# Spreading a decode-attention kernel's softmax steps over three units of work, with small products and copies moved to ScalarE

## The chip, the cores and the metric

The kernel runs on one core of one Trainium2 chip. The metric is the device time of one execution in microseconds (us); each kernel has several runs. A run comes with the span of its profile (first to last instruction), the granted TensorE clock, and a state: "slow" when it is over 1.5% above the fastest run of the same kernel. "TensorE" does the matrix products, "VectorE" and "ScalarE" the elementwise work; in profile lines they are PE (with PEld for weight loads), DVE and ACT. SP is the engine that only issues the large transfers.

## The reference, cut to what matters

Eight sequences (batch 8), one new token each. Attention with 16 query heads on 8 key/value heads of width 256 over the last 1024 cached positions, beside a small MLP, mixed by a gate:

```python
q = (x @ wq) ...                                  # 8 x 16 heads x 256
scores = einsum("bhqd,bhkd->bhqk", q, k) * Dh**-0.5
p = softmax(scores);  o = einsum("bhqk,bhkd->bhqd", p, v)
a = o.reshape(B, Sq, Hq*Dh) @ wo
b = gelu(layernorm(x) @ w1 + b1) @ w2 + b2
return g * a + (1 - g) * b                        # g = sigmoid(sum(x * gate_w))
```

The cached keys and values are by far the largest input: 67 MB of 77.7 MB.

## The kernel before

Work is cut into 16 units (`NQ`): four key/value heads of one sequence each. A unit needs a 2 MB slot of keys and a 2 MB slot of values, which arrive in a ring of nine slots, in the order of use. A slot's buffer can be refilled when its last reader is done. Per unit: VectorE transposes the keys in four pieces (two halves of two); TensorE makes the scores in two halves of eight matmuls; the row maximum is found and shared (`top`, `share`); ScalarE takes exp; VectorE transposes the result (`turn`); TensorE multiplies with the values (`values`), and the result is combined (`gather`) and brought into place (`finish`). The excerpt leaves out allocations and bookkeeping.

```python
def turn(u):
    E, rowsum = soft.pop(u)
    ET = opool.tile(...)
    nc.vector.transpose(ET..., E...)
    selr = epool.tile([P, RQ], F32, ...)
    nc.vector.tensor_scalar_mul(selr[:], sel[:], rowsum[:])
    sm = ps_sm.tile([P, RQ], F32, tag="sm", name="sm")
    nc.tensor.matmul(sm[:], lhsT=ones_f[:], rhs=selr[:], start=True, stop=True)

def invert(u):
    nc.vector.reciprocal(rb[:], sm[:])
    nc.vector.tensor_tensor(rsel[:], rb[:], sel2[:], op=ALU.mult)

def gather(u):
    nc.vector.tensor_scalar_mul(os_[:], PO[:, 0, :], own[:, 0:1])
    nc.vector.scalar_tensor_tensor(os_[:], in0=PO[:, 1, :], scalar=own[:, 1:2],
                                   in1=os_[:], op0=ALU.mult, op1=ALU.add)

def finish(u):
    for j in range(NJ):
        nc.tensor.matmul(sm[:, j, :], lhsT=os_[:, j::NJ], rhs=rsel[:], ...)
    nc.vector.tensor_copy(oT[...], sm[:])          # the "oT copy"

# ... the start: MLP weights, then query weights; then
hs = mlp_hidden()
query()
for hf in range(NH):
    scores(0, hf)
mlp_out(hs)                                        # ends with a VectorE product, mixb
for u in range(1, NQ):
    for piece in range(CH // PIECE):
        turn_keys(u, 0, piece)
    scores(u, 0)
    top(u - 1)
    turn_keys(u, 1, 0)
    share(u - 1)                                   # with exp on ScalarE
    turn_keys(u, 1, 1)
    if u >= LAG:
        values(u - LAG)
    scores(u, 1)
    turn(u - 1)
    if u >= LAG:
        gather(u - LAG)
    invert(u - 1)
    if u >= LAG:
        finish(u - LAG)
# ... the last unit, then the projection with wo, and the output
```

This is the order in which each engine is given its instructions.

## Time and profile before

| | before |
|---|---|
| time, median of 3 runs | 211.6 us (211.46 to 214.57) |
| span of the profile | 210.8 us |
| busy: TensorE, VectorE, ScalarE | 140.1, 148.1, 29.7 us |
| mean granted TensorE clock | 0.83 of full |
| bytes moved, and rate in the loop | 77.7 MB, 2 MB slot each 4.89 us (428 GB/s) |
| last packet of the weights | 186.6 us |

From the page's part 2, the kernel before: each digit is the busy share, in tenths, of one of 40 slices of 5.3 us; PEclk is the granted TensorE clock in tenths of full.

```profile
PE   0069629575958676595959595958595858673771
DVE  7876140949697979979797979796969687883320
PEclk9999999858888789978888887879797969696555
DMA  5999999999999999999999999999999999910000
```

The transfers look like the limit: nine tenths and more until slice 35. But after them comes a tail of 24 us, in which only computing is left. So computing is behind. The chain of waits (the work that ended last, followed backwards; columns are start, length, engine, what was written, source line) shows one unit of the loop, kernel before:

```profile
168.60 2.24 DVE kt L358 x2
170.88 3.37 PE S L431 x8
174.40 0.17 DVE nmx L453
174.66 1.47 ACT E L456 x2
176.15 0.71 DVE ET L469
176.98 0.40 DVE os__1435 L506
177.40 0.50 DVE os__1435 L507
177.94 0.65 PE sm L522 x4
178.62 0.23 DVE oT L525
178.84 2.24 DVE kt L358 x2
```

From 168.60 to 178.84 us it is 10.24 us. The second line's first half of the scores (`S`, eight matmuls) takes 3.37 us, 0.42 us per matmul; the second half, off this chain, takes 1.91, 0.24 per matmul. The view of stretches tells why; its columns are the stretch, TensorE's busy time, weight loads, VectorE, ScalarE, GpSimd, then granted clock, DMA share and GB/s. Kernel before, three windows of 3.41 us and the next:

```profile
119.28:122.69 3.41, 3.00 (x8) 1.03 (x8) 2.84 (x4) 0.00 (x0) 0.00 (x0) 0.50 0.99 416
122.69:126.11 3.42, 2.99 (x27) 1.45 (x27) 2.45 (x5) 1.47 (x2) 0.00 (x0) 1.00 1.02 436
126.11:129.52 3.41, 1.37 (x9) 0.97 (x8) 2.96 (x7) 0.00 (x0) 0.00 (x0) 1.00 1.02 432
129.52:132.93 3.41, 2.99 (x8) 1.02 (x8) 2.85 (x4) 0.00 (x0) 0.00 (x0) 0.50 0.97 413
```

In the third window TensorE works 1.37 of 3.41 us, with one pause of 2.31 us that begins in it; in the fourth the clock is at half, and all eight score matmuls of the half unit begin in it. The trace's clock records repeat 6.83 us at full and 3.41 us at half: together 10.24 us, the pitch of the loop. From here on "window" is only a name for a stretch of 3.41 us (the lengths of these records, but for the last, are multiples of it), "gate", in the recorded texts, for the falls of the granted clock to 0.50, and "warm" and "cold" mean granted 1.00 and 0.50. Why the clock falls the records don't say.

### The profile page before, as it was taken

How to read it: one execution, taken by the hardware profiler on the slowest of the kernel's cores; microseconds unless marked ns; L12 is line 12 of the kernel's file. 1: busy time of each engine (PE TensorE's matmuls, PEld its weight loads, DVE VectorE, ACT ScalarE, POOL GpSimd, SP SyncE). 2: the span in 40 equal slices, each digit the busy share in tenths (PEclk: the TensorE clock that was granted, in tenths of full speed). 3: DMA queues.
4: the chain of work that ended last, by engine and by line, in shares of the span. 5: the costliest groups of instructions: out<-in, count | busy, mean ns of one | idle time of the engine just before them, and what ended most of it. 6: DMA issues, size and time to landing. Idle time of an engine off the chain costs nothing.

```text
span 210.8 us, 2528 instructions
## 1 busy us (share of the span) xinstructions
PE 140.1 (66%) x1013; PEld 70.6 (34%) x1022; DVE 148.1 (70%) x282; ACT 29.7 (14%) x40; POOL 0.8 (0%) x7
## 2 busy tenths in 40 slices
PE   0069629575958676595959595958595858673771
PEld 0066304231524333332324242424141424232361
DVE  7876140949697979979797979796969687883320
ACT  2210220020202112020202020202020202022000
POOL 1000000000000000000000000000000000000000
PEclk9999999858888789978888887879797969696555
DMA  5999999999999999999999999999999999910000
GB/s 225 411 437 420 432 420 431 429 420 435 423 429 435 417 438 420 429 432 423 429 429 423 434 426 417 441 417 429 435 423 435 432 410 418 404 54 0 0 3 4
DMA packets 6733, 77.84 MB, mean 369 GB/s; under 512 B 945, under 2 KB 1346, under 8 KB 1986
## 3 DMA queue, kind: packets, MB, share of 16 engines
q1 hardware_dynamic: 6512, 77.67, 87.1%
q8 instruction: 7, 0.11, 0.2%
q10 hardware_dynamic: 210, 0.02, 0.1%
q14 instruction: 4, 0.03, 0.0%
HBM read 77.68 MB, written 0.01 MB: 368 GB/s over the span
## 4 chain that ended last, share of the span: by engine, by line
PE 46%; DVE 38%; ACT 10%; issue 3%; ACTq 0%
PE S L431 27%; DVE kt L358 17%; ACT E L456 8%; PE sm L522 5%; DVE ET L469 4%; PE PO L493 3%; DVE oT L525 2%; PE Sq L374 2%; PE A_ps L656 1%; PE hT L545 1%; PE hT L535 1%; PE mz L451 1%; DVE qw L416 1%; DVE nmx L453 1%; DVE mx L443 1%
## 5 line engine op out<-in xcount | busy, mean ns | idle before, releaser
L431 PE MATMUL S<-kt,qw 128*128 128x512 bf16 x256 | 81.9, 476 | 44.2 <-DVE kt L358 39.2
L358 DVE STREAM_TRANSPOSE kt<-slot 128x1024 int32<-128x1024 int32 x64 | 77.1, 1226 | 0.0
L431 PEld LDWEIGHTS <-qw 128*128 128x128 bf16 x256 | 28.7, 112 | 86.8 <-issue 67.8
L456 ACT ACTIVATE E<-S,nmx 128x1024 bf16<-128x1024 f32 x16 | 22.6, 1412 | 140.1 <-DVE nmx L453 140.1
L493 PE MATMUL PO<-slot,ET 128*16 128x512 bf16 x256 | 20.2, 444 | 0.0
L443 DVE TENSOR_REDUCE mx<-S 128x1 f32<-128x1024 f32 x16 | 19.0, 1187 | 0.0
L469 DVE STREAM_TRANSPOSE ET<-E 128x512 int32<-128x512 int32 x16 | 11.4, 711 | 8.0 <-ACT E L456 8.0
L453 DVE TENSOR_REDUCE nmx<-mz 128x1 f32<-128x4 f32 x16 | 2.6, 160 | 12.9 <-PE mz L451 12.9
L451 PEld LDWEIGHTS mz<-m,same 128*128 128x128 f32 x32 | 7.4, 235 | 6.6 <-issue 3.9
L425 PE MATMUL S<-place,foreign 128*128 128x512 bf16 x23 | 9.2, 400 | 0.0
L476 PEld LDWEIGHTS sm<-selr,ones_f 128*128 128x128 f32 x32 | 6.4, 204 | 5.3 <-issue 3.1
L525 DVE CAST oT<-sm 128x16 bf16<-128x16 f32 x16 | 3.6, 226 | 6.3 <-PE sm L522 6.2
L493 PEld LDWEIGHTS <-ET 128*16 128x16 bf16 x256 | 5.6, 95 | 5.5 <-issue 2.7
L425 PEld LDWEIGHTS <-foreign 128*128 128x128 bf16 x32 | 4.8, 149 | 7.0 <-issue 6.9
L476 PE MATMUL sm<-selr,ones_f 128*128 128x8 f32 x32 | 4.9, 226 | 2.7 <-DVE selr L474 2.7
L451 PE MATMUL mz<-m,same 128*128 128x4 f32 x32 | 5.1, 230 | 1.7 <-DVE m L445 1.7
L482 DVE RECIPROCAL rb<-sm 128x8 f32<-128x8 f32 x16 | 3.3, 207 | 3.7 <-PE sm L476 3.6
L595 DVE TENSOR_SCALAR mixb<-bb,gg_s 128x112 f32<-128x112 f32 x1 | 0.3, 333 | 6.4 <-PE bb L591 6.4
L241 PE MATMUL tp<-ident,y_sb 8*128 8x8 bf16 x3 | 0.2, 170 | 6.9 <-DVE y_sb L302 6.9
L416 DVE CAST qw<-qp 32x1024 bf16<-32x1024 f32 x2 | 2.4, 1224 | 2.9 <-ACT qw L414 2.9
L445 DVE TENSOR_SCALAR m<-block,mx 128x4 f32<-128x4 f32 x16 | 3.7, 229 | 0.6
L374 PE MATMUL Sq<-slot,xT 128*8 128x512 bf16 x32 | 3.7, 621 | 0.0
(152 smaller groups left out, 93.8 us busy)
## 6 DMA issues: line engine op xcount, KB each, us to landing
slot<-in_A_v_cache_dram SPq DMA_DIRECT2D x16, 2048.0 KB, 24.9
slot<-in_A_k_cache_dram SPq DMA_DIRECT2D x15, 2048.0 KB, 29.4
slot<-in_A_wo_dram SPq DMA_DIRECT2D x3, 896.0 KB, 19.3
slot<-in_A_k_cache_dram SPq DMA_DIRECT2D x2, 1024.0 KB, 7.1
slot<-in_A_wq_dram SPq DMA_DIRECT2D x1, 2048.0 KB
slot<-in_B_w_dram SPq DMA_DIRECT2D x1, 1568.0 KB
slot<-in_B_w_dram SPq DMA_DIRECT2D x1, 1344.0 KB, 9.8
slot<-in_A_wq_dram SPq DMA_DIRECT2D x1, 1024.0 KB
```

What stands on the lines that cost most here:

```text
L358: nc.vector.transpose(KT[u, hf][:, c0 : c0 + PIECE] .rearrange("p c k x r -> p (c k x r)") .bitcast(WORD), kn[:, o : o + PIECE * Dh].bitca ...
L374: nc.tensor.matmul(Sq[32 * t : 32 * t + NB, n * QN : (n + 1) * QN], lhsT=xT[:, r + half, :], rhs=w[:, o + c : o + c + QN], start=(r == 0), ...
L425: nc.tensor.matmul(S[u][:, cols], lhsT=foreign[:], rhs=place[:], start=True, stop=False)
L431: nc.tensor.matmul(S[u][:, cols], lhsT=qw[:, j, u, m * RQ : m * RQ + P], rhs=kt[:, :, k, :, par], start=False, stop=(k == NK - 1 and par = ...
L443: nc.vector.reduce_max(mx[:], S[u][:], axis=AXIS.X)
L451: nc.tensor.matmul(mz[:], lhsT=same[:], rhs=m4[:], start=True, stop=True)
L456: nc.scalar.activation(E[:].rearrange("p c x i -> p c i x"), S.pop(u)[:].rearrange("p (c i x) -> p c i x", i=PAIR, x=BLK), ACT.Exp, bias=n ...
L469: nc.vector.transpose(ET[:].rearrange("p c r i -> p (c r i)").bitcast(WORD), E[:].rearrange("p c x i -> p (c x i)").bitcast(WORD),)
L476: nc.tensor.matmul(sm[:], lhsT=ones_f[:], rhs=selr[:], start=True, stop=True)
L493: nc.tensor.matmul(PO[32 * t : 32 * t + PAIR * RQ], lhsT=ET[:, c, 0:RQ, :], rhs=vn[:, PAIR * c * Dh : PAIR * (c + 1) * Dh], start=(c < QUA ...
L522: nc.tensor.matmul(sm[:, j, :], lhsT=os_[:, j::NJ], rhs=rsel[:], start=True, stop=True)
L525: nc.vector.tensor_copy(oT[:, half * RQ : (half + 1) * RQ, :, b].rearrange("p h j -> p j h"), sm[:])
```

## The change

Its intent: take VectorE work out of the unit, spread one unit's softmax over three (scores in unit u, exp at the end of u+1, its transpose in u+2, combining in u+3), so that no engine waits for a step just started; and start the query earlier. The core of the diff:

```diff
     add_kv("k", A_k_cache, 0, parts=2)
-    add(("w1",), rows_loader([w1_m, w1_t]))
     add(("wq", 0), ...)
     add(("wq", 1), ...)
+    add(("w1",), rows_loader([w1_m, w1_t]))
...                                            # keys transposed in one piece per half
-        selr = ...; nc.vector.tensor_scalar_mul(selr[:], sel[:], rowsum[:])
-        nc.tensor.matmul(sm[:], lhsT=ones_f[:], rhs=selr[:], ...)
+        nc.tensor.matmul(den[u][:], lhsT=rowden[:], rhs=rowsum[:], ...)     # total()
...
-        nc.vector.reciprocal(rb[:], sm[:])                                  # 128x8
-        nc.vector.tensor_tensor(rsel[:], rb[:], sel2[:], op=ALU.mult)
+        nc.vector.reciprocal(rb[:], den.pop(u)[:])                          # 128x1
+        nc.scalar.activation(rsel[u][:], sel2[:], ACT.Copy, scale=rb[:])
...
+        nc.scalar.activation(first[:], PO[:, 0, :], ACT.Copy, scale=own[:, 0:1])  # in values()
-        nc.vector.tensor_scalar_mul(os_[:], PO[:, 0, :], own[:, 0:1])
...
-        nc.vector.tensor_copy(oT[...], sm[:])
+        nc.scalar.copy(oT[...], sm[:])
...
-        nc.vector.tensor_scalar_mul(mixb[:], bb[:], gg_s[:, 1:2])
+        nc.scalar.activation(mixb[:], bb[:], ACT.Copy, scale=gg_s[:, 1:2])
...
-    hs = mlp_hidden()
     query()
+    hs = mlp_hidden()
...
     for u in range(1, NQ):
+        turn_keys(u, 0); scores(u, 0)
+        gather(u - LAG - 1); turn(u - LAG); total(u - LAG); finish(u - LAG - 1)
+        top(u - 1); share(u - 1)                   # the shared maximum, without exp
+        turn_keys(u, 1); values(u - LAG); invert(u - LAG)
+        scores(u, 1)
+        expo(u - 1)                                # exp
```

Also, the large clearing of `qw` moves to GpSimd, and the query's copies are split into eight.

More of the change, by code (lines that the diff above doesn't have):

```diff
@@ L77 @@
     BLK = 32
-    PIECE = 8
     BIG = 1e30
@@ L195 @@
     make_identity(nc, ident[:])
-    ones_f = consts.tile([P, P], F32)
-    nc.gpsimd.memset(ones_f[:], 1.0)
     Sq = ps_s.tile([P, W], F32, tag="S", name="Sq")
@@ L217 @@
     yT = consts.tile([P, NX, NB], BF16)
-    sel = consts.tile([P, RQ], F32)
+    rowden = consts.tile([P, P], F32)
     sel2 = consts.tile([P, RQ], F32)
@@ L250 @@
     by_row = ident[:].rearrange("p (b r) -> p r b", b=QUAD)
-    nc.vector.reduce_sum(sel[:], by_row[:, 0:RQ, :], axis=AXIS.X)
     nc.vector.reduce_sum(block[:], by_col, axis=AXIS.X)
@@ L257 @@
         zrow[:].rearrange("p (o r) -> p o r", o=1).to_broadcast([P, QUAD, BLK]),
+    )
+    nc.vector.tensor_copy(
+        rowden[:].rearrange("p (b r i) -> p b r i", b=QUAD, i=PAIR),
+        zrow[:, 0 : BLK // PAIR]
+        .rearrange("p (o r v) -> p o r v", o=1, v=1)
+        .to_broadcast([P, QUAD, BLK // PAIR, PAIR]),
     )
@@ L288 @@
             )
-    nc.vector.memset(qw[:], 0.0)
+    nc.gpsimd.memset(qw[:], 0.0)
     def norm_and_gate():
@@ L348, with turn_keys @@
     KT = {}
-    def turn_keys(u, hf, piece):
+    def turn_keys(u, hf):
         kn = slot("k", u)
-        if piece == 0:
-            KT[u, hf] = ktpool.tile(
-                [P, CH, NK, BLK, NPAR], BF16, tag="kt", name="kt"
-            )
-        c0 = piece * PIECE
-        o = (hf * CH + c0) * Dh
+        kt = ktpool.tile([P, CH, NK, BLK, NPAR], BF16, tag="kt", name="kt")
+        KT[u, hf] = kt
         nc.vector.transpose(
-            KT[u, hf][:, c0 : c0 + PIECE]
-            .rearrange("p c k x r -> p (c k x r)")
-            .bitcast(WORD),
-            kn[:, o : o + PIECE * Dh].bitcast(WORD),
+            kt[:].rearrange("p c k x r -> p (c k x r)").bitcast(WORD),
+            kn[:, hf * CH * Dh : (hf + 1) * CH * Dh].bitcast(WORD),
         )
-        if (hf + 1) * CH == NCK and c0 + PIECE == CH:
+        if hf == NH - 1:
             done()
@@ L410, in query @@
             rows = slice(BLK * b, BLK * (b + 1))
-            dst = qw[rows, :, :, BLK * b : BLK * (b + 1)]
-            src = qp[rows].rearrange("p j u m q -> p j u (m q)")
-            if b % 2 == 0:
-                nc.scalar.copy(dst, src)
-            else:
-                nc.vector.tensor_copy(dst, src)
+            for j in range(NJ):
+                dst = qw[rows, j, :, BLK * b : BLK * (b + 1)]
+                src = qp[rows, j].rearrange("p u m q -> p u (m q)")
+                if j == 0:
+                    nc.scalar.copy(dst, src)
+                else:
+                    nc.vector.tensor_copy(dst, src)
     S = {}
@@ L451, in share, with expo @@
         nc.tensor.matmul(mz[:], lhsT=same[:], rhs=m4[:], start=True, stop=True)
+        soft[u] = mz
+    def expo(u):
+        mz = soft.pop(u)
         nmx = epool.tile([P, 1], F32, tag="nmx", name="nmx")
@@ L467, in turn @@
         E, rowsum = soft.pop(u)
-        ET = opool.tile([P, NCK // PAIR, BLK, PAIR], BF16, tag="ET", name="ET")
+        ET = epool.tile([P, NCK // PAIR, BLK, PAIR], BF16, tag="ET", name="ET")
         nc.vector.transpose(
@@ L472, in turn, with total @@
         )
-        selr = epool.tile([P, RQ], F32, tag="selr", name="selr")
-        nc.vector.tensor_scalar_mul(selr[:], sel[:], rowsum[:])
-        sm = ps_sm.tile([P, RQ], F32, tag="sm", name="sm")
-        nc.tensor.matmul(sm[:], lhsT=ones_f[:], rhs=selr[:], start=True, stop=True)
-        soft[u] = (ET, sm)
-    def invert(u):
-        ET, sm = soft.pop(u)
-        rb = epool.tile([P, RQ], F32, tag="rb", name="rb")
-        nc.vector.reciprocal(rb[:], sm[:])
-        rsel = opool.tile([P, RQ], F32, tag="rsel", name="rsel")
-        nc.vector.tensor_tensor(rsel[:], rb[:], sel2[:], op=ALU.mult)
-        soft[u] = (ET, rsel)
+        soft[u] = (ET, rowsum)
+    den = {}
+    def total(u):
+        ET, rowsum = soft.pop(u)
+        den[u] = ps_sm.tile([P, 1], F32, tag="sm", name="den")
+        nc.tensor.matmul(
+            den[u][:], lhsT=rowden[:], rhs=rowsum[:], start=True, stop=True
+        )
+        soft[u] = ET
+    rsel = {}
+    def invert(u):
+        rsel[u] = opool.tile([P, RQ], F32, tag="rsel", name="rsel")
+        rb = epool.tile([P, 1], F32, tag="rb", name="rb")
+        nc.vector.reciprocal(rb[:], den.pop(u)[:])
+        nc.scalar.activation(rsel[u][:], sel2[:], ACT.Copy, scale=rb[:])
     def values(u):
-        ET, rsel = soft.pop(u)
+        ET = soft.pop(u)
         vn = slot("v", u)
@@ L500, in values @@
         done()
-        soft[u] = rsel
+        first = epool.tile([P, Dh], F32, tag="first", name="first")
+        nc.scalar.activation(first[:], PO[:, 0, :], ACT.Copy, scale=own[:, 0:1])
+        soft[u] = first
     def gather(u):
-        rsel = soft.pop(u)
+        first = soft.pop(u)
         os_ = epool.tile([P, Dh], F32, tag="os", name="os_")
-        nc.vector.tensor_scalar_mul(os_[:], PO[:, 0, :], own[:, 0:1])
         nc.vector.scalar_tensor_tensor(
@@ L510, in gather @@
             scalar=own[:, 1:2],
-            in1=os_[:],
+            in1=first[:],
             op0=ALU.mult,
@@ L514, in gather @@
         )
-        soft[u] = (os_, rsel)
+        soft[u] = os_
     def finish(u):
         b, half = divmod(u, Hkv // QUAD)
-        os_, rsel = soft.pop(u)
-        sm = ps_sm.tile([P, NJ, RQ], F32, tag="sm", name="sm")
+        os_, rs = soft.pop(u), rsel.pop(u)
+        sm = ps_sm.tile([P, NJ, RQ], F32, tag="sm", name="fin")
         for j in range(NJ):
             nc.tensor.matmul(
-                sm[:, j, :], lhsT=os_[:, j::NJ], rhs=rsel[:], start=True, stop=True
+                sm[:, j, :], lhsT=os_[:, j::NJ], rhs=rs[:], start=True, stop=True
             )
-        nc.vector.tensor_copy(
+        nc.scalar.copy(
             oT[:, half * RQ : (half + 1) * RQ, :, b].rearrange("p h j -> p j h"), sm[:]
@@ L594, in mlp_out @@
         done()
-        nc.vector.tensor_scalar_mul(mixb[:], bb[:], gg_s[:, 1:2])
+        nc.scalar.activation(mixb[:], bb[:], ACT.Copy, scale=gg_s[:, 1:2])
     norm_and_gate()
     for hf in range(NH):
-        for piece in range(CH // PIECE):
-            turn_keys(0, hf, piece)
+        turn_keys(0, hf)
+    query()
     hs = mlp_hidden()
-    query()
     for hf in range(NH):
@@ L606 @@
     for u in range(1, NQ):
-        for piece in range(CH // PIECE):
-            turn_keys(u, 0, piece)
+        turn_keys(u, 0)
         scores(u, 0)
+        if u >= LAG + 1:
+            gather(u - LAG - 1)
+        if u >= LAG:
+            turn(u - LAG)
+            total(u - LAG)
+        if u >= LAG + 1:
+            finish(u - LAG - 1)
         top(u - 1)
-        turn_keys(u, 1, 0)
         share(u - 1)
-        turn_keys(u, 1, 1)
+        turn_keys(u, 1)
         if u >= LAG:
             values(u - LAG)
+            invert(u - LAG)
         scores(u, 1)
-        turn(u - 1)
-        if u >= LAG:
-            gather(u - LAG)
-        invert(u - 1)
-        if u >= LAG:
-            finish(u - LAG)
+        expo(u - 1)
     u = NQ - 1
+    turn(u - 1)
+    total(u - 1)
     top(u)
     share(u)
+    gather(u - 2)
+    finish(u - 2)
+    invert(u - 1)
+    expo(u)
+    values(u - 1)
     turn(u)
-    values(u - 1)
+    total(u)
+    invert(u)
     gather(u - 1)
-    invert(u)
     A_ps = ps_misc.tile([P, DO], F32, tag="misc", name="A_ps")
```

## The prediction

The forecast's sum: 162.6 + 10 + 16 us is about 188.5 for the projection's end; with 0.4 and 4.1 the span is 193, and with 0.8 the time is 194 us. Two figures of its work per unit are estimates. The 2.26 us of a merged transpose is a straight line through the trace's 0.71 and 1.23 us (measured in the changed kernel: 2.31). ScalarE's added 1.0 us was measured there as 0.47 + 0.30 + 0.23 us (half of the combining, rsel, oT copy).

> **What bounds the kernel now.** The timeline shows a steady loop of 10.24 us per unit (score matmuls of successive units start at 119.69 and 129.94 us). The chain of waits runs through it serially: two key transposes 2.24, scores 3.37, sharing the maximum, exp 1.47, E transpose 0.71, combining 0.9, finishing 0.65, copy 0.23, then the next transposes. VectorE is busy about 8.9 of the 10.24 us; the rest is waiting inside this chain. The first eight score matmuls run 427 ns apart, the second eight 239 ns: TensorE stands idle 2.3 us before them and is halved for the next 3.41 us window (granted clock about 0.83). [...]10.24 us is exactly three windows.
>
> Under it lies a floor. The DMA row is at nine tenths until 184 us; a 2 MB slot takes 4.89 us (428 GB/s[...]). Two slots per unit are 9.79 us. All 77.7 MB land by about 186 us, and nothing the change does moves that. Unit 15's keys land at about 162 us but are transposed only at 178.8: the loop starts at 37 us (keys landed at 29) and loses 0.45 us per unit. So the prize is the 24 us after the last byte.
>
> **What the change does, per unit.** VectorE loses: the selr product 0.19, rsel product 0.17, first half of combining 0.48, the oT copy 0.23, and a fixed part of each merged transpose (1.23 for 1024 words, 0.71 for 512, so about 2.26 for 2048 against 2.45: 0.4 in all). Sum 1.4: 8.9 becomes 7.5 us. ScalarE gains about 1.0 us (estimate: one 128x256, two small operations) on 1.6. More important, the order: exp is started at a unit's end and its result transposed only one half later; gathering and finishing move one unit on. No VectorE step then waits for a fresh exp or finish. Compute alone could go at about 7.5 to 8.5 us per unit, below the 9.79 us of DMA.
>
> **Start.** Query weights first: queries need wq, landing about 4 us earlier, and no longer wait for the MLP; unit 1 starts near 30 us instead of 37. Compute catches up within about five units and then waits for keys.
>
> **End.** Unit 15 starts near 162.6; its iteration takes about 10, the epilogue (two value steps, finishes, spreading, 3.1 us of projection) about 16, so projection ends near 188.5; the last weights land at 186 to 187. Then 0.4 us and the 4.1 us of output seen now: span about 193. Runs read about 0.8 us above the span: **194 us**, range **191 to 200**.
>
> Chances: faster 0.96, same 0.03, slower 0.01.
>
> **What would show it.** DMA still at nine tenths and about 428 GB/s to about 186 us, with only some 6 to 8 us after it; VectorE transposes now waiting for the key slots' DMA, 1 to 2 us per unit from about unit 4 on; starts of units 9.8 us apart late, about 8 early; VectorE busy near 120 us; landing times from issue up towards 34 us.
>
> **What would make it wrong.** The halved clock: if TensorE's waits for DMA keep one window in three cold, and a cold score half plus the shared maximum (it waits for ScalarE's oT copy for its PSUM buffer) exceeds 9.8 us, the loop locks again at 10.24 us: then about 202.

## More of the kernel before

One more line matters, from the groups (line, engine, operation, count, busy us and mean ns, idle time just before and its releaser). Kernel before:

```profile
L595 DVE TENSOR_SCALAR mixb<-bb,gg_s 128x112 f32<-128x112 f32 x1 | 0.3, 333 | 6.4 <-PE bb L591 6.4
```

VectorE stands 6.4 us before the loop to make one 0.3 us product for the MLP.

## The result, and the profile after

The changed kernel's median was 195.28 us (4 runs, 192.88 to 196.14, two of them slow) against 211.53 us before. The ratio is 0.9165, 95% interval 0.9068 to 0.9262. Here and below a ratio is the mean time of one kernel's fast runs over that of the other's in the same rounds, so it isn't quite the ratio of the medians.

The same rows of part 2, changed kernel (40 slices of 4.8 us):

```profile
PE   0035999794878489857666699859684999396773
DVE  7876465995949494949493949494949585865310
PEclk9999657999699966999999558979998599997558
DMA  5999999999999999999999999999999999999980
```

The transfers now run almost to the end, and VectorE's row alternates. What it waits for is in the waits (engine, line, releaser: total us, times, longest us), changed kernel:

```profile
DVE kt L356 <- DMA slot<-in_A_k_cache_dram: 35.8, 14, 3.0
```

The timeline of VectorE has two successive units; the bracket is the idle time and its releaser:

```profile
133.91 2.31 DVE L356 STREAM_TRANSPOSE kt<-slot 128x2048 int32<-128x2048 int32 x1 [2.40 <-DMA slot<-in_A_k_cache_dram]
...
143.69 2.31 DVE L356 STREAM_TRANSPOSE kt<-slot 128x2048 int32<-128x2048 int32 x1 [2.79 <-DMA slot<-in_A_k_cache_dram]
```

The pitch is 9.78 us, two slots of 4.89 us. Each unit starts when its keys land. The start of the first key transposes of some units, read from the two traces, in us:

| unit | 1 | 2 | 3 | 6 | 10 | 15 | last projection matmul | span |
|---|---|---|---|---|---|---|---|---|
| keys landed (changed) | 29.4 | 34.4 | 44.2 | 73.7 | 112.9 | 162.1 | (weights: 186.3) | |
| before | 37.3 | 48.0 | 58.0 | 86.6 | 127.5 | 178.7 | 206.4 | 210.8 |
| changed | 31.0 | 36.8 | 45.6 | 75.0 | 114.3 | 163.3 | 187.9 | 191.1 |

The landing row is worked out from the packet records, adding up their bytes in order. By unit 3 the changed kernel is only 1.4 us behind the keys, and stays about there. The chain that ended last is the transfers up to unit 15, then the end of the kernel:

```profile
124.17 39.13 DMA slot<-in_A_k_cache_dram
163.31 2.32 DVE kt L356
...
184.87 3.00 PE A_ps L671 x126
187.89 0.33 DVE res L688
```

The last projection matmul ends 1.6 us after the weights' last packet. So the 24 us tail has become 5 us.

### The profile page after: what moved, and what is told of

The parts are those of the page before. It is cut to its first block, busy times and chain, and to the rows that moved or that the text cites. A ratio compares the mean times of both kernels' runs of the same rounds, so it can differ in the third digit from the quotient of the medians.

```text
span 191.1 us, 2508 instructions
## 1 busy us (share of the span) xinstructions
PE 135.0 (71%) x1022; PEld 69.5 (36%) x1022; DVE 128.0 (67%) x186; ACT 43.1 (23%) x91; POOL 5.0 (3%) x7
## 4 chain that ended last, share of the span: by engine, by line
DMA 84%; PE 7%; DVE 3%; ACT 3%; SPq 1%; issue 1%
DMA slot<-in_A_k_cache_dram 77%; DMA slot<-in_A_wq_dram 7%; PE fin L530 2%; PE A_ps L671 2%; ACT E L457 1%; PE PO L500 1%; DVE kt L356 1%; PE S L428 1%; DVE ET L470 1%; SPq L118 1%; DVE mx L440 1%; ACT first L509 0%; PE mz L448 0%; ACT oT L533 0%; PE pp L655 0%
## 5 line engine op out<-in xcount | busy, mean ns | idle before, releaser
L356 DVE STREAM_TRANSPOSE kt<-slot 128x2048 int32<-128x2048 int32 x32 | 73.7, 2305 | 35.8 <-DMA slot<-in_A_k_cache_dram 35.8
L428 PE MATMUL S<-kt,qw 128*128 128x512 bf16 x256 | 71.0, 424 | 29.9 <-DVE kt L356 27.6
L533 ACT CAST oT<-fin 128x16 bf16<-128x16 f32 x16 | 3.6, 227 | 82.2 <-PE fin L530 82.2
L509 ACT ACTIVATE first<-PO,own 128x256 f32<-128x256 f32 x16 | 7.6, 473 | 28.6 <-PE PO L500 28.5
L422 PE MATMUL S<-place,foreign 128*128 128x512 bf16 x32 | 13.4, 418 | 0.1
L481 PEld LDWEIGHTS den<-rowsum,rowden 128*128 128x128 f32 x32 | 7.2, 231 | 4.5 <-issue 1.4
L481 PE MATMUL den<-rowsum,rowden 128*128 128x1 f32 x32 | 5.2, 233 | 0.0
L492 ACT ACTIVATE rsel<-sel,rb 128x8 f32<-128x8 f32 x16 | 4.7, 296 | 0.7 <-DVE rb L491 0.7
L413 DVE CAST qw<-qp 32x512 bf16<-32x512 f32 x4 | 2.7, 687 | 3.2 <-ACT qw L411 3.2
L291 POOL MEMSET qw<- 128x5120 bf16 x1 | 4.4, 4364 | 0.0
## 6 DMA issues: line engine op xcount, KB each, us to landing
slot<-in_A_v_cache_dram SPq DMA_DIRECT2D x16, 2048.0 KB, 36.8
```

The costliest lines, as they stand in the source:

```text
L291: nc.gpsimd.memset(qw[:], 0.0)
L356: nc.vector.transpose(kt[:].rearrange("p c k x r -> p (c k x r)").bitcast(WORD), kn[:, hf * CH * Dh : (hf + 1) * CH * Dh].bitcast(WORD),)
L422: nc.tensor.matmul(S[u][:, cols], lhsT=foreign[:], rhs=place[:], start=True, stop=False)
L428: nc.tensor.matmul(S[u][:, cols], lhsT=qw[:, j, u, m * RQ : m * RQ + P], rhs=kt[:, :, k, :, par], start=False, stop=(k == NK - 1 and par = ...
L481: nc.tensor.matmul(den[u][:], lhsT=rowden[:], rhs=rowsum[:], start=True, stop=True)
L492: nc.scalar.activation(rsel[u][:], sel2[:], ACT.Copy, scale=rb[:])
```

## The experiments

Eleven kernels ran, in three groups; each group shares its runs of the kernel before, on one chip (medians before: 211.47, 213.0 and 213.05 us). The record's verdict is "faster" for e1, e5, e6, e7 and e8, "same" for e4, "unclear" for the third group (e9 to e11), in which five of the eleven runs of the kernel before were slow, and none for the single runs e2 and e3. All results passed the comparison with the reference. That says little for two of them (e2 and e3), which are wrong and passed too: the comparison doesn't resolve that part.

### e1: the changed kernel again

No edit.

> The changed kernel once more, unaltered, to see its spread and what moves in it. My theory (it is held by the transfers): unit starts 9.79 us apart from unit 3 on, last slot landed at about 186 us, span 191 to 194.5, times 192.5 to 196.5. A rival (its loop is still held by compute, which only happens to be near 9.8 us): in some runs the pitch differs from 9.79 us and vector transposes don't wait for key slots.

Measured: 194.37 us median (4 runs, 192.52 to 195.67), ratio 0.9175. From unit 3 on the pitch was 9.78 to 9.80 us, the last packet at 186.4, the last projection matmul at 187.5. The result repeats, with a spread of 3 us that e10 and e11 look into.

### e2 and e3: a quarter of the values, in both kernels

```diff
-        n = NCK * Dh // parts
+        n = NCK * Dh // parts // cut            # cut = 4 for values, 1 for keys
...
-        rhs=vn[:, PAIR * c * Dh : PAIR * (c + 1) * Dh],
+        rhs=vn[:, PAIR * t * Dh : PAIR * (t + 1) * Dh],     # t = c % 4
```

The work of the engines stays the same; the transfers shrink from 77.7 to 52.5 MB.

> The changed kernel, loading only a quarter of each value slot (and using that quarter four times; the result is wrong on purpose). Per unit the transfers then need about 6.1 us instead of 9.79. Theory (transfers hold the changed kernel; its compute alone goes at 7.5 to 8.5 us per unit): pitch falls to 7.5 to 8.5 us, unit 15 starts near 143 us, time about 171 us (167 to 178). Rival (compute holds it near 9.8 us): time stays above 190 us.

> The kernel before with the same cut of the value slots (wrong on purpose). Theory (its loop of 10.24 us is a chain of computing steps, and the transfers, though nine tenths busy, don't hold it): pitch stays 10.24 us, time 209 to 214 us. Rival (its transfers at nine tenths hold it): the time falls by 10 us or more.

Measured, e2: one run, 155.14 us (state unknown). The pitch fell to 6.90 us, below the 7.5 to 8.5 us I had expected. Part 2 and VectorE's timeline of e2:

```profile
DVE  7987524599999999999999999999999999663200
PEclk9999999999999999999999999999999999997558
...
91.58 2.29 DVE L356 STREAM_TRANSPOSE kt<-slot 128x2048 int32<-128x2048 int32 x1
98.48 2.29 DVE L356 STREAM_TRANSPOSE kt<-slot 128x2048 int32<-128x2048 int32 x1
```

VectorE is busy 6.86 of the 6.90 us, and in the loop TensorE's clock stays full. The transfers are not what holds e2: unit 15's keys landed at 114.7 us and were first transposed at 126.1. So 6.90 us per unit is the changed kernel's own pace, and the 9.79 us of the real one are the transfers'.

Measured, e3: one run, 214.75 us, span 213.0, clock 0.809 (state unknown). That is longer than any uncut run on its chip (spans of 208.1 to 211.3 us). The trace shows where: from unit 2 on its pitch was never under 10.2 us, where the profiled run of the kernel before had pitches of 9.05 to 10.02 us between units 2 and 6. Uncut runs had spans of 212.8 to 213.0 us at clock 0.809 or 0.810 five times, on other chips; the record calls those slow. That the cut adds nothing is likely, but one run doesn't show it. The chain of e3:

```profile
140.14 2.24 DVE kt L358 x2
142.42 3.38 PE S L431 x8
...
150.38 2.24 DVE kt L358 x2
```

The same stretch of both kernels in the view of stretches (columns as above), first the kernel before, then e3:

```profile
139.90:150.20 10.30, 7.34 (x41) 3.45 (x42) 8.34 (x15) 1.45 (x2) 0.00 (x0) 0.83 1.00 423
```

```profile
139.90:150.20 10.30, 7.74 (x43) 3.46 (x42) 8.32 (x15) 1.45 (x2) 0.00 (x0) 0.83 0.63 241
```

With 241 instead of 423 GB/s the pitch is still 10.24 us, and the clock still 0.83, though unit 15's keys landed at 145.9 us, 35 us before their use. A DMA row at nine tenths wasn't what held the kernel before.

### e4: the kernel before, query first

```diff
+    add(("wq", 0), ...); add(("wq", 1), ...)
     add(("w1",), ...)
-    add(("wq", 0), ...); add(("wq", 1), ...)
...
-    hs = mlp_hidden()
     query()
+    hs = mlp_hidden()
```

> The kernel before with only the start of the change: query weights loaded and query computed ahead of the MLP. Theory: unit 1 starts about 5 to 7 us earlier (30 to 32 us instead of 37), the loop keeps its 10.24 us, and as nothing catches the transfers up, all of it is gained at the end: 204 to 207 us. Rival (the start is hidden, only the loop counts): 211 us.

Measured: 210.94 us median, ratio 0.9974 (0.9913 to 1.0035): the same. My theory fell here. Unit 1 started at 35.2 us instead of 37.3, because VectorE still waited for the MLP's last matmuls to make `mixb`, the line shown above. Of those 2.1 us, 1.3 were left at unit 15 (177.4 us), with the pitch at 10.24 from unit 7 on.

### e5: the changed kernel, MLP first

The reverse edit, on the changed kernel.

> The changed kernel with only its start undone: MLP weights and MLP first, then the query. Theory (transfers hold it, and its compute alone needs 6.9 us per unit, as the run with a quarter of the values showed): unit 1 starts some 5 us later, near 36 to 38 us, catches up at 2.9 us per unit within three or four units, and unit 15 still starts near 163.4: time within 1 us of the changed kernel's, 193 to 196. Rival (the earlier start is worth its 5 us): 198 to 201.

Measured: 193.66 us median (6 runs, 192.55 to 196.46), ratio 0.9062 (0.8976 to 0.9148), not slower than the changed kernel's 0.9165 and 0.9175. Unit 1 started at 30.8 us, as in the changed kernel (I had expected 36 to 38); unit 2 at 40.3 instead of 36.8; by unit 4 both were at the pace of the keys. So the query's place is not what starts unit 1 early. With e4 this leaves `mixb`, which in the changed kernel and e5 is on ScalarE. The traces support it: VectorE's last step ahead of that point, the clearing of `bb`, starts at 30.44 us in the kernel before and at 30.55 us in e5. Only `mixb` then stands between it and unit 1's keys, which start at 37.3 and 30.8 us. Moving `mixb` alone wasn't run.

### e6: new order, old division of work

The changed kernel, with VectorE making again what it made in the loop before. The start stays the changed one, `mixb` on ScalarE included. The diff is shortened:

```diff
+        selr = ...; nc.vector.tensor_scalar_mul(selr[:], sel[:], rowsum[:])
...
-        nc.scalar.activation(rsel[u][:], sel2[:], ACT.Copy, scale=rb[:])
+        nc.vector.tensor_tensor(rsel[u][:], rb[:], sel2[:], op=ALU.mult)
...
+        nc.vector.tensor_scalar_mul(os_[:], PO[:, 0, :], own[:, 0:1])
...
-        nc.scalar.copy(oT[...], sm[:])
+        nc.vector.tensor_copy(oT[...], sm[:])
...                                            # keys in two pieces per half again
-    finish(u - 2); invert(u - 1)
+    invert(u - 1); finish(u - 2)              # at the end only
```

The last swap was a precaution. I expected a deadlock without it: three products in a row ask for the two buffers of one pool, and with the copy on VectorE the step that frees one comes after that copy in VectorE's order. No run shows it.

> The changed kernel's order and start, but the old division of work: VectorE makes the selr product, the rsel product, both halves of the combining and the oT copy, and transposes keys in two pieces each. Theory (order alone is enough): VectorE's 6.9 us per unit grow by about 1.4 to 8.3, plus up to 0.8 of waiting for the finishing matmuls; still under 9.79, so the pitch is 9.79 and the time 193 to 198. Rival (relieving VectorE is what counts): pitch near 10.24, time 205 or more.

Measured: 198.41 us median (198.08 to 199.15), ratio 0.9339 (0.9279 to 0.9398). The pitch was 9.79 us from unit 9 on, and unit 15 started at 163.7 us, as in the changed kernel. The new order, with the changed start, brings the loop to the keys' pace, barely. VectorE now waits mostly for the finishing matmuls, and only 5.6 us in all for keys (columns as in the waits above):

```profile
DVE oT L534 <- PE fin L531: 21.0, 16, 2.5
DVE kt L356 <- DMA slot<-in_A_k_cache_dram: 5.6, 7, 1.8
```

The remaining time is in the end: from unit 15's start to the last projection matmul it took 29.4 us instead of the changed kernel's 24.6. It seems that in the end, with no transfers to hide behind, every VectorE step counts; that wasn't tested apart, and the swapped end is part of it.

### e7: old order, new division of work

The edits of e6 the other way, on the kernel before (the transposed exp gets two buffers rather than three).

> The kernel before in its old order and start, with only the work moved to ScalarE (half of the combining, rsel, oT copy) and the row sums spread by one matrix product. Theory (order is what counts, the chain within a unit stays): about 1.0 us of VectorE work leaves the chain, but exp, its transpose and the cold score half stay in it; pitch 9.2 to 10.24 us, time 199 to 211. Rival (relieving VectorE is enough): pitch 9.79 or less from early on, time 193 to 197.

Measured: 194.87 us median (194.42 to 195.32), ratio 0.9167 (0.9108 to 0.9226): by the ratios, as fast as the whole change. My theory that order counts and work doesn't fell here. The pitch went 8.26, 9.6, 9.3 and round again, 9.07 us on average (46.8 to 164.7 us over 13 units), without a single wait for keys: it started late, at 36.3 us, and at unit 15 was still 2.7 us behind the landing of the keys (162.0 us). The old chain is still there, but the fixed lock on 10.24 us is gone.

### e8: the kernel before, kept warm

```diff
+    def keep_warm(n):
+        wm = ps_misc.tile([P, QN], F32, tag="misc", name="wm")
+        for _ in range(n):
+            nc.tensor.matmul(wm[:], lhsT=foreign[:], rhs=place[:]..., start=True, stop=True)
...
             finish(u - LAG)
+        keep_warm(8)
```

Eight products nobody reads, in each unit's pause; all else as before.

> The kernel before, with eight matmuls into an unused PSUM bank at the end of each unit, where TensorE stands idle 2.3 us. Nothing else changes; results stay right. Rival theory (it is the halved clock that holds the loop at 10.24 us, three gate windows; the change works because it ends that lock): the first score half takes 1.9 us instead of 3.37, the granted clock is 1.0 in the loop, the pitch falls by 1.4 to about 8.8 us of compute, so that the transfers hold it at 9.79, and the time falls to 194 to 200 us. Theory of order alone (the chain would be nearly as long warm): 205 us or more.

Measured: 195.95 us median (195.31 to 197.04), ratio 0.9223 (0.9156 to 0.929). The clock row and TensorE's timeline of e8:

```profile
PEclk9999966969999999999999999999999999999558
...
135.85 1.89 PE L600 MATMUL wm<-place,foreign 128*128 128x512 bf16 x8
138.54 1.90 PE L431 MATMUL S<-kt,qw 128*128 128x512 bf16 x8 [0.58 <-DVE kt L358]
```

The first half of the scores takes 1.90 us instead of 3.37, the pitch is 9.04 us, and unit 15 starts at 163.6 us, 15 us earlier than before. Adding 120 useless matmuls won nearly all that the change wins. It was the halved clock that made 10.24 us out of 9.04.

### e9: the kernel before, one copy moved

```diff
-        nc.vector.tensor_copy(oT[...], sm[:])
+        nc.scalar.copy(oT[...], sm[:])
```

> The kernel before with one line changed: ScalarE instead of VectorE makes the small oT copy that ends each unit. In the kernel before, VectorE starts the next unit's key transposes only after that copy, and the copy waits for the finishing matmuls. Theory (a small shortening of TensorE's 2.3 us pause at the unit's end is enough to break the lock on three gate windows): the transposes start about 0.6 us earlier relative to the finishing matmuls, TensorE's pause falls to about 1.8 us, the pitch leaves 10.24 us and falls to 9.0 to 9.8 us, time 194 to 203 us. Rival (the lock holds[...]): pitch 10.24 us, time 209 us or more.

Measured: 201.58 us median (200.12 to 202.86), ratio 0.9532 (0.9438 to 0.9626). The timeline of e9: the next unit's key transposes now start 0.45 us before the copy.

```profile
131.89 2.36 DVE L358 STREAM_TRANSPOSE kt<-slot 128x1024 int32<-128x1024 int32 x2
132.34 0.23 ACT L525 CAST oT<-sm 128x16 bf16<-128x16 f32 x1 [2.49 <-PE sm L522]
134.30 3.12 PE L431 MATMUL S<-kt,qw 128*128 128x512 bf16 x8 [1.77 <-DVE kt L358]
```

TensorE's pause fell from 2.3 to 1.77 us and the pitch to 9.43 us on average (46.9 to 169.5 us over 13 units), in turns of 8.5, 9.6 and 9.9. The lock broke, though some units still meet a halved clock, as this one does. By the ratio, moving a 0.23 us copy was worth 4.7%; the record's verdict on the time is "unclear", but unit 15 starts at 169.5 us in the trace, 9.2 us earlier than before.

### e10 and e11: the end reordered, and kept warm

e10 is the changed kernel with the last value matmuls ahead of unit 14's finish:

```diff
-    finish(u - 1)
+    values(u); finish(u - 1); gather(u); finish(u)
     ...
     spread_rows(0, HALF)
-    values(u); gather(u); finish(u)
     spread_rows(HALF, NHQ)
```

e11 adds nine idle matmuls in two pauses of the end.

> The changed kernel with only the end reordered: the last unit's value matmuls go ahead of unit 14's finishing matmuls, so that both finishes and both spreadings stand together ahead of the projection. Theory (compute's end was at 187.5 to 189.5 us, 1.2 to 3.2 us after the last byte's 186.4; about 1.5 us of it were serial waits here): projection ends at 187.3 to 188 us, held by the last weights, and the times come out at 192 to 194.5, about half a per cent to one under the changed kernel's 194 to 195. Rival (the end is held by the last transfer already): same time within 0.3 per cent.

> As the run with the reordered end, and nine idle matmuls into an unused bank in the end's two longest pauses of TensorE (six ahead of sharing the last maximum, three ahead of the last denominators). Theory (the spread of the changed kernel, 192.5 to 196.5 us, comes from the gate halving TensorE's clock at different places of the end): the times bunch nearer 192 to 193.5 us and projection ends near 187.5 us. Rival (the spread comes from the transfers or from elsewhere): spread as before.

Measured, e10: 192.25 us median (6 runs, 192.01 to 193.71), ratio 0.9106 (0.9054 to 0.9157). e11: 192.23 us (6 runs, 192.08 to 192.95), ratio 0.9095 (0.9053 to 0.9137). The chain of e10 at its end:

```profile
168.07 18.54 DMA slot<-in_A_wo_dram
186.65 0.30 PE A_ps L674 x8
186.97 0.33 DVE res L688
```

Now only the eight matmuls of the last piece of weights come after its transfer. These have the lowest medians; the spread shrank from 3 us to 1.7 and 0.9. They did not run on one chip with the changed kernel, so only ratios to the kernel before compare them, and the intervals overlap (e5's ratio, with the end unchanged, is lower still). In the chain the projection ends 0.8 us after the last packet (186.2), against 1.6 in the changed kernel and 1.1 in e1; that this is what lowers the time is likely, but not shown. The clock did differ in the end: by the view of stretches it was 0.50 from 174.3 to 187.8 us in the changed kernel, but 1.00 from 174.0 to 180.5 in e11, and 0.50 from 181 to 187; in e10 it was 1.00 from 170 to 175 and 0.55 from 175.4 to 186.9. What the warmth alone is worth beyond the order is not settled, as e10 has the same median.

## Why the prediction was right, point by point

- **The floor.** "All 77.7 MB land by about 186 us, and nothing the change does moves that": last packet at 186.3 us; the pitch is 9.79 us as said, and e2 shows that it is the transfers' pitch.
- **The total.** Span about 193 and time 194 us were predicted; the profiled span was 191.1, and the median 195.28 us. That the time came so close is partly luck, as errors cancelled. The profiled run was the fastest of four, at 192.88 us, and in it the end was shorter (3.2 us from the last product to the end of the span, where I had counted 4.5; projection ended at 187.9 instead of 188.5), but runs read 1.8 us above the span, not 0.8. I had taken 0.8 from a median and a profile of different runs; the profiled run of the kernel before read 213.03 us, 2.2 above its span. The rest of the way up to the median is the spread of the runs, which I had not forecast.
- **Own pace of computing.** "7.5 to 8.5 us per unit" was too slow: e2 measured 6.90. VectorE fell from 148.1 to 128.0 us, not to "near 120": the merged transposes won less than the 0.4 us per unit I gave them (77.1 to 73.7 us in all, 0.2 per unit). What I had missed is that I added up durations: in one unit of e2 those of VectorE's eight steps add up to 7.42 us, close to my 7.5, but by the trace six of the seven handovers overlap by 0.07 to 0.09 us, and the pitch is 6.90. Hence waits for keys of 1.7 to 3.0 us, 2.6 on average, rather than "1 to 2".
- **The start.** "Unit 1 starts near 30 us" was right (31.0) for a wrong reason. The step that failed is "Query weights first ... unit 1 starts near 30 us instead of 37": e4 gained 2.1 us of it, and e5, without it, started at 30.8. VectorE's 6.4 us wait for `mixb` was on the page; I didn't weigh it.
- **What the gain came from.** I read the halved clock as part of the chain, and priced the change by the chain's and VectorE's length. The experiments show that the kernel before had a way to 9.04 us without either: only the halved clock held it at 10.24. New order with the new start (e6), new work (e7) or idle products (e8) each bring the loop to or below the keys' 9.79 us. Past that, the change's other savings in the loop are paid out in waiting for keys, 35.8 us of it.
- **The feared lock** of the changed kernel at 10.24 us didn't come: in e2, without waits for transfers, its clock stays full; with them it varies (0.86 to 0.89 in the mean of the fast runs), but 6.9 us of work have room in 9.79.

Paces and ends in one table (pitch in the later loop; e2 and e3 with a quarter of the values):

| kernel | pitch, us | unit 15 starts, us | median, us |
|---|---|---|---|
| before | 10.24 | 178.7 | 211.5 to 213.1 |
| e3 before, quarter values | 10.24 | 181.0 | 214.75 |
| e4 query first | 10.24 | 177.4 | 210.94 |
| e9 one copy moved | 9.43 mean | 169.5 | 201.58 |
| e7 new work only | 9.07 mean | 164.7 | 194.87 |
| e8 kept warm | 9.04 | 163.6 | 195.95 |
| e6 new order only | 9.79 | 163.7 | 198.41 |
| changed | 9.79 | 163.3 | 195.28 and 194.37 |
| e5 changed, MLP first | 9.79 | 163.5 | 193.66 |
| e2 changed, quarter values | 6.90 | 126.1 | 155.14 |
| e10 end reordered | 9.79 | 163.2 | 192.25 |
| e11 end reordered and warm | 9.79 | 163.4 | 192.23 |

## What to carry to other kernels

These are lessons of this one kernel. A transfer row at nine tenths doesn't prove that transfers hold a kernel: cut the bytes and see whether the pitch moves, and look for compute that trails the landing times. When a loop's pitch is that of its clock records, as here with 6.83 us full and 3.41 half in 10.24, test a few idle matmuls in TensorE's pause before you redesign anything (eight a unit gave 9.04 us in e8); a shorter pause (1.77 us instead of 2.3 in e9, by moving a 0.23 us copy) may be worth more than less work. And once the loop reaches the transfers' pace, further savings count only after the last byte: e5's later unit 2 and e8's later start were caught up by unit 15.

## What the clock records show

- In the profiled run of the kernel before, a window with 1.37 of 3.41 us of matmuls, and no pause over 2.31 us, was followed by the half clock, and so were its like (1.34 to 1.38 us), one in each unit from 95 us to the end of the loop. Counted from the clock records and matmul times of the two profiled runs, before and changed, over 64 full-clock windows: the 19 with at most 1.44 us of matmuls were each followed by the half clock, the 40 with at least 1.75 us by the full one. Of the five from 1.50 to 1.70 us, three were followed by the half clock, two by the full one. The experiments' traces aren't in this count, and it says nothing of the cause.
- This loop repeated with the records: 6.83 us full and 3.41 us half, pitch 10.24 us, where the same work kept warm takes 9.04 (e8).
